# Batch 3's k turned by the transposing DMA in a kernel of sliding-window attention and a feed-forward layer

## The chip, the core and the metric

The kernel runs on one core of a Trainium2 chip. The core has a TensorE (PE in the profile; its weight loads are PEld), a VectorE (DVE), a ScalarE (ACT), a GpSimd (POOL) and a SyncE (SP), which here does nothing but issue DMAs. Each engine works off its own list of instructions in order; they meet through semaphores. SBUF is the on-chip memory, PSUM the banks that TensorE writes into. The metric is the device time of one execution in microseconds (us), as the median of several runs.

## What is computed

Eight batches, eight heads, 576 tokens, 64 values a head. Attention looks back over a window of 128 tokens with a linear bias that differs by head; its output, 4608 tokens of 512 values, is the x of a feed-forward layer.

```python
scores = scale * np.matmul(q, k.transpose(0, 1, 3, 2))
mask = (rel >= 0) & (rel < 128)                 # rel = row position - column position
scores = np.where(mask, scores + bias[None], -1000000000.0)
attn = softmax(scores)
x = np.matmul(attn, v)                          # then heads side by side: 4608 x 512
h = x @ w_in                                    # 512 x 2048
g = h * np.clip(h + 3.0, 0.0, 6.0) / 6.0
out = g @ w_out                                 # 2048 x 512, float32
```

Inputs and output are float32; matmuls take bfloat16.

## The kernel before

Attention goes in steps of two heads of one batch. A step has the number g: batch g // 4, pair g % 4, so g runs from 0 to 31. The feed-forward layer goes in nine tiles of 512 tokens. Its units are "ups" (`moe_up`: four matmuls over the four head pairs of x^T, then a Relu on ScalarE into `r6` and a multiplication on VectorE into `gbuf`) and "downs" (`moe_down`: four of the sixteen matmuls of a 128-token output block; after the fourth unit VectorE copies the block to `osb`, and SP writes it out). `fill(n)` places up to n of these units between the parts of an attention step. The order of every engine's instructions is written out by hand: the program stands in a manual schedule, and instructions run on each engine in the order in which the Python code issues them. An up whose tile needs a batch that is not yet finished is held back when the program is built (`done`), so which unit stands where is fixed too.

Scores need q and k with the head's values on the partitions: `qTb` and `kTb`, two buffers each, taken by turns by even and odd batches. x is needed the same way round: `xT`. There are two ways to turn something round:

- By TensorE: `double` transposes nine 128x128 blocks of a pair of head pairs (five, then four) from a cast copy `pr` into PSUM, and an engine copies the result into `qTb` or `kTb`.
- By the DMA: `xbar` (line 200) is one transposing DMA of 20 blocks from the cast copy `tbuf`; `back` (line 476) is one of five blocks from `avs`, the normalised output of a step, into `xT`. All of them are issued by SP, in line with the loads of q, k and v (line 112, five DMAs for a tensor of one batch) and the writes of the output (line 562).

From step 8 on, the loop in `segment` runs one iteration for each g. Iteration g issues scores of step g, with the masks and exponentials of g, the product of step g - 1 with v (`values`), the turning of g - 1's output (`back`), feed-forward units in between, and last `stage_next(g)`, which loads, casts and turns for the next batch. (Step 13's scores come at the end of iteration 12.) So q and k of batch 3 are got ready in iterations 8 to 11, those of batch 4 in 12 and 13.

Batch 3 is the odd one out. Its q is loaded in token order, cast by GpSimd into `tbuf` (iteration 9) and turned by one transposing DMA. Its k is loaded in runs of nine tokens (`load_double`), cast by GpSimd into two `pr` tiles in iterations 8 and 9 (`prepare_double`), and turned by TensorE in iterations 10 and 11: the dictionary `turn` in `segment` calls `double` twice in each, with a copy on ScalarE after each of the two parts. From batch 4 on, q and k are both cast into `tbuf`, q in the first iteration of the batch before and k in the second, and turned by one transposing DMA each; k's cast has to wait until q's turn has read `tbuf`.

SP's list around the change, from iteration 9 on, is: an output block; x^T of step 8; v of batch 3 (five loads); q of batch 3 turned; an output block; x^T of step 9; q of batch 4 (five loads); three output blocks; k of batch 4 (five loads); q of batch 4 turned; x^T of step 12; v of batch 4 (five loads); k of batch 4 turned; an output block; x^T of step 13; q of batch 5 (five loads); an output block; x^T of step 14; an output block; x^T of step 15; k of batch 5; and so on. (Steps 10 and 11 are turned back by TensorE.)

The tile 3 of the feed-forward layer is the first that needs batch 3. Its first up stands in iteration 17, after the scores of step 17, and reads x^T of steps 12 to 15.

Of the kernel before, what the change touches and what calls it, by code (L numbers as in the profile page):

```python
# [11 lines left out]
BF16 = mybir.dt.bfloat16  # L12
# [6 lines left out]
def kernel(  # L19
# [9 lines left out]
    nc = tc.nc  # L29
    B, H, S, D = q.shape  # L30
# [5 lines left out]
    NP = H // 2  # L36
    NQ = 5
# [3 lines left out]
    RP, RT = 64, 9  # L41
# [21 lines left out]
    bias_o = perm.tile([128, H], FP32)  # L63

    held = ctx.enter_context(tc.tile_pool(name="held", bufs=1))
    prs = ctx.enter_context(tc.tile_pool(name="prs", bufs=2))
    ppool = ctx.enter_context(tc.tile_pool(name="ppool", bufs=2))
    small = ctx.enter_context(tc.tile_pool(name="small", bufs=2))
    rpool = ctx.enter_context(tc.tile_pool(name="rpool", bufs=2))
# [4 lines left out]
    ps_o = ctx.enter_context(tc.tile_pool(name="ps_o", bufs=1, space=bass.MemoryType.PSUM))  # L74

    tbuf = held.tile([128, NP, NQ, 128], BF16, name="tbuf")
    ldbuf = [held.tile([128, NQ * H * D], FP32, name=f"ldbuf{i}") for i in range(4)]
    gbuf = [held.tile([128, n_ms, NT], BF16, name=f"gbuf{i}") for i in range(2)]
    vbuf = [held.tile([128, NQ, H, W], BF16, name=f"vbuf{i}") for i in range(2)]
    p4buf = [held.tile([128, 2, 128], BF16, name=f"p4buf{i}") for i in range(2)]  # L80
    qTb = [held.tile([128, NP, NQ, 128], BF16, name=f"qTb{i}") for i in range(2)]
    kTb = [held.tile([128, NP, NQ, 128], BF16, name=f"kTb{i}") for i in range(2)]
# [19 lines left out]
    def tokens(b, nm):  # L102
        if (b, nm) not in ld:
            i = 2 + b % 2 if b < 3 else (3, 1, 0, 2)[(3 * (b - 3) + "qkv".index(nm)) % 4]
            ld[b, nm] = ldbuf[i][:, 0:NQ * H * D].rearrange("p (j h d) -> p j h d", j=NQ, h=H)
        return ld[b, nm]

    def load_tokens(b, nm):
        t = tokens(b, nm)
        for j in range(NQ):  # L110
            n = min(128, S - j * 128)
            nc.sync.dma_start(out=t[:n, j, :, :],
                              in_=src_of[nm][b, :, ds(j * 128, n), :].rearrange("h p d -> p h d"))
# [66 lines left out]
    def cast_v(b, j, copy):  # L180
        n = min(128, S - j * 128)
        copy(out=vbuf[b % 2][:n, j, :, 0:D], in_=ld[b, "v"][:n, j, :, :])

    def cast_tokens(b, nm):
        s = ld[b, nm]
        if nm == "v":
            for lo in (0, 2):
                nc.gpsimd.tensor_copy(  # L188
                    out=vbuf[b % 2][:, lo:lo + 2, :, 0:D].rearrange("p j h d -> p (j h) d"),
                    in_=s[:, lo:lo + 2, :, :].rearrange("p j h d -> p (j h) d"))  # L190
            nc.gpsimd.tensor_copy(out=vbuf[b % 2][:LAST, 4, :, 0:D], in_=s[:LAST, 4, :, :])
            return
        for j in range(NQ):
            m = min(128, S - j * 128)
            nc.gpsimd.tensor_copy(out=tbuf[:m, :, j, :],  # L195
                                  in_=s[:m, j, :, :].rearrange("p (i e) d -> p i (e d)", e=2))

    def xbar(b, nm):
        dst = (qTb if nm == "q" else kTb)[b % 2]
        nc.sync.dma_start_transpose(out=dst.rearrange("p h j c -> p (h j) c"),  # L200
                                    in_=tbuf.rearrange("p h j c -> p (h j c)"))

    st = {}

    def prepare(g, copies):
        for nm, copy in zip("qk", copies):
            pr = prs.tile([128, RT * D], BF16, tag=f"pr{nm}", name="pr",
                          padded_shape=[128, 2 * RT * D])
            copy(out=pr, in_=runs[nm][:, g % NP, :])
            st[g, nm] = pr  # L210

    def transposes(g, copies):
        b, hp = divmod(g, NP)
        for nm, dst, copy in (("q", qTb[b % 2], copies[0]), ("k", kTb[b % 2], copies[1])):
            src = st.pop((g, nm))
            tp = ps_h.tile([128, RT, RP], BF16, tag="h", name="tp", padded_shape=[128, 16, 64])
            for t in range(RT):
# [3 lines left out]
            copy(out=dst[:, hp, :, :].rearrange("p j c -> p (j c)")[:, 0:S].rearrange(  # L221
                "p (a t) -> p a t", t=RT), in_=tp.rearrange("p t a -> p a t"))

    def prepare_double(b, dp, copies, nms="kq", early=None):
        for nm, copy in zip(nms, copies):
            pr = prs.tile([128, RT, 2 * D], BF16, tag=f"pr{nm}", name="pr2")
            for e in range(2):
                copy(out=pr[:, :, ts(e, D)],  # L228
                     in_=ldbuf["qk".index(nm)][:, ds((2 * dp + e) * RT * D, RT * D)].rearrange(
                         "p (t d) -> p t d", t=RT))  # L230
                if early and (nm, e) == (nms[0], 0):
                    early()
            st[b, dp, nm] = pr
# [3 lines left out]
    def double(b, dp, nm, part, tag, copy):  # L237
        src = st[b, dp, nm]
        t0, t1 = ((0, 5), (5, RT))[part]
        tp = BANKS[tag].tile([128, t1 - t0, 128], BF16, tag=tag, name="tp2",  # L240
                             padded_shape=[128, 8, 128])
        for t in range(t0, t1):
            nc.tensor.transpose(tp[:, t - t0, :], src[:, t, :], ident)  # L243
        dst = (qTb if nm == "q" else kTb)[b % 2][:, 2 * dp:2 * dp + 2, :, :]
        copy(out=dst.rearrange("p i j c -> p i (j c)")[:, :, 0:S].rearrange(  # L245
                 "p i (a t) -> p i a t", t=RT)[:, :, :, t0:t1],
             in_=tp.rearrange("p t (a i) -> p i a t", i=2))

    def wide_double(b, dp, nm, copy):
# [195 lines left out]
    def values(g, qts):  # L445
        av = ps_av.tile([128, 3, 2, W], FP32, tag="av", name="av", padded_shape=[128, 3, 2, 85])
        nq = len(qts)
        av_matmuls(g, qts, lambda qt, e: av[:, qt - qts[0], e, :])
        if qts[0] == 0:
            st[g, "avs"] = small.tile([128, NQ, 2, D], BF16, tag="avs", name="avs")  # L450
        rc = small.tile([128, 3, 2, 1], FP32, tag="rc", name="rc")
        nc.vector.reciprocal(rc[:, 0:nq, :, :], av[:, 0:nq, :, D:W])
        nc.vector.tensor_tensor(  # L453
            out=st[g, "avs"][:, qts[0]:qts[0] + nq, :, :], in0=av[:, 0:nq, :, 0:D],
            in1=rc[:, 0:nq, :, :].to_broadcast([128, nq, 2, D]), op=ALU.mult)
# [13 lines left out]
    def by_xbar(g):  # L469
        return g >= XB and g != XB + 2 and g != XB + 3  # L470
# [103 lines left out]
    def fill(n):  # L574
        for _ in range(n):
            if at[0] == len(units):
                return
            nt, fn, step = units[at[0]]
            if fn is moe_up and done[0] < NP * (min((nt * NT + NT - 1) // S, B - 1) + 1):
                return  # L580
            fn(nt if fn is moe_up else nt - 1, step)
            at[0] += 1

    V, P, A = nc.vector.tensor_copy, nc.gpsimd.tensor_copy, nc.scalar.copy

    LOADS = {9: "v3", 10: "q4", 12: "k4", 13: "v4", 14: "q5", 16: "k5", 17: "v5", 18: "q6",
             20: "k6", 21: "v6", 22: "q7", 24: "k7", 25: "v7"}

    VCAST = {15: 4, 19: 5, 23: 6, 27: 7}

    def stage_next(g):
        b, hp = divmod(g, NP)
        nb = b + 1
        if g == 2 * NP:
            cast_tokens(2, "v")
        for n in LOADS.get(g, "").split():
            load_tokens(int(n[1]), n[0])
        if nb == 3 and hp < 2:
            prepare_double(3, hp, (P,), "k")
        if nb == 3 and hp == 1:  # L600
            cast_tokens(3, "q")
            xbar(3, "q")
        elif nb < B and nb > 3 and hp < 2:
            cast_tokens(nb, "qk"[hp])
            xbar(nb, "qk"[hp])
        if VCAST.get(g):
            cast_tokens(VCAST[g], "v")

# [109 lines left out]
    def segment(lo, hi, fills):  # L718
        for g in range(lo, hi + 1):
            f = fills(g)  # L720
            if by_xbar(g - 2):
                done[0] = g - 1
            if lo < g < hi and g != 3 * NP + 1:
                scores(g)
            turn = {2 * NP: (2, 1, "k"), 2 * NP + 1: (2, 1, "q"),
                    2 * NP + 2: (3, 0, "k"), 2 * NP + 3: (3, 1, "k")}.get(g)
            if turn:
                double(*turn, 0, "av", A)
            fill(f[0])
            if turn:  # L730
                double(*turn, 1, *(("h", V) if turn[0] == 2 else ("av", A)))
            if g < hi:
                exp_diag(g, 0)
            fill(f[1])
            if g < hi:
                exp_diag(g, 1)
            if g == 3 * NP:
                cast_tokens(3, "v")
            if g > lo:
                values(g - 1, (0, 1, 2))  # L740
            fill(f[2])
            if g < hi:
                exp_off(g, 0)
            fill(f[3])
            if g < hi:
                exp_off(g, 1)
            if g > lo:
                values(g - 1, (3, 4))
            fill(f[4])
            if g > lo and by_xbar(g - 1):  # L750
                back(g - 1)
            fill(f[5])
            if g < hi:
                stage_next(g)
            fill(1)
            if g == 3 * NP:
                scores(g + 1)
            if g > lo and not by_xbar(g - 1):
                back(g - 1)
                done[0] = g  # L760
            fill(f[6] - 1)
# [51 lines left out]
```

## Time and profile before

| what | us |
|---|---|
| median of 3 runs | 321.99 |
| lowest and highest of them | 320.54, 322.87 |
| the profiled execution: time | 320.94 |
| the profiled execution: span of the instructions | 319.2 |
| PE busy | 310.1 |
| ACT busy | 195.7 |
| DVE busy | 173.1 |
| POOL busy | 141.2 |

The profiled execution took 1.7 us more than its span, which lies around the first and the last instruction, and 1.05 us less than the median of the runs. The profile counts a PE as busy while matmuls are in flight, so its share says that something was under way, not that the array worked at its peak. A line of the timeline gives the start and the length in us, the engine, the source line, the operation, the tile written and the tiles read, and how many instructions were merged. SP's lines are marked SPq: their length is the time for which SP was occupied with issuing the DMA, not the time until the data had landed, which another view gives ("DMA to landing", counted from the start of the issue).

### The profile page before, as it was taken

What the parts mean: (1) busy time and instruction counts of PE and PEld (TensorE: products, weight loads), DVE (VectorE), ACT (ScalarE), POOL (GpSimd) and SP (SyncE); (2) the same over time, 40 slices, a digit from 0 to 9 for tenths busy, and PEclk for the clock granted to TensorE, in tenths of its full rate; (3) what the DMA queues carried; (4) which work ended last, traced back from release to release, by engine and by line L of the source; (5) the groups of instructions that cost most, each with busy time, mean ns of one, the idle gap of its engine ahead of it and who ended that gap; (6) DMA issues with size and microseconds to landing.
All of it is one profiled execution on the core that took longest, in us unless ns stands there. A gap on an engine that the chain in (4) does not pass through costs nothing.

```text
span 319.2 us, 7124 instructions
## 1 busy us (share of the span) xinstructions
PE 310.1 (97%) x2775; PEld 164.9 (52%) x2775; DVE 173.1 (54%) x338; ACT 195.7 (61%) x334; POOL 141.2 (44%) x249
## 2 busy tenths in 40 slices
PE   7879999999999999999999999999999999999996
PEld 5565465455545454445677654444444444444443
DVE  6667675554355655655565556555656455455510
ACT  4748976877767776676676667666764344244401
POOL 8464493684496477266744673663331000000000
PEclk9999999999999999999999999999999999999999
DMA  7999999999999999998999999962212110000112
GB/s 281 199 323 225 256 260 195 249 231 194 215 252 157 239 208 211 205 222 194 207 205 211 209 190 196 225 93 68 38 39 88 53 36 33 33 33 35 66 56 75
DMA packets 131425, 51.90 MB, mean 163 GB/s; under 512 B 118976, under 2 KB 123328, under 8 KB 131392
## 3 DMA queue, kind: packets, MB, share of 16 engines
q1 hardware_dynamic: 126160, 45.36, 68.0%
q0 software_dynamic: 4224, 4.19, 8.2%
q10 hardware_dynamic: 1008, 1.90, 1.6%
q8 instruction: 21, 0.34, 0.5%
q14 instruction: 12, 0.10, 0.1%
HBM read 36.70 MB, written 9.44 MB: 145 GB/s over the span
## 4 chain that ended last, share of the span: by engine, by line
PE 86%; DMA 5%; ACT 4%; POOL 2%; DVE 2%; issue 1%; POOLq 0%
PE ops L552 38%; PE hps L502 36%; DMA w_in_sb<-in_moe_w_in_dram 3%; PE sce L365 3%; PE av L442 2%; PE av L434 2%; DMA ldbuf<-in_k_dram 2%; ACT r L521 2%; PE ops L533 1%; ACT kTb L245 1%; ACT gbuf L399 1%; PE tp L243 1%; DVE gbuf L522 0%; ACT gbuf L377 0%; PE tb L483 0%
## 5 line engine op out<-in xcount | busy, mean ns | idle before, releaser
L522 DVE SCALAR_TENSOR_TENSOR gbuf<-r,hps 128x512 bf16<-128x512 f32 x144 | 98.7, 688 | 101.0 <-ACT r L521 99.8
L521 ACT ACTIVATE r<-hps,bias 128x512 f32<-128x512 f32 x144 | 98.9, 689 | 86.8 <-PE hps L502 86.6
L502 PE MATMUL hps<-xT,w_in_sb 128*128 128x512 bf16 (+1 forms) x640 | 144.9, 358 | 0.6 <-ACT xT L489 0.3
L552 PE MATMUL ops<-w_out_sb,gbuf 128*128 128x512 bf16 x560 | 137.8, 379 | 0.0
L502 PEld LDWEIGHTS <-w_in_sb 128*128 128x128 bf16 x640 | 59.3, 98 | 55.0 <-issue 0.8
L552 PEld LDWEIGHTS <-gbuf 128*128 128x128 bf16 x560 | 51.9, 98 | 56.3
L415 POOL TENSOR_SCALAR_AFFINE_SELECT po<-po 128x512 bf16<-128x512 bf16 x48 | 30.3, 636 | 32.5 <-ACT po L413 32.4
L406 POOL TENSOR_SCALAR_AFFINE_SELECT pd<-pd 128x512 bf16<-128x512 bf16 x48 | 29.8, 634 | 33.5 <-ACT pd L389 33.5
L389 ACT ACTIVATE pd<-sce,bias_d 128x512 bf16<-128x512 f32 x48 | 31.7, 684 | 5.4 <-PE sce L373 2.7
L561 DVE COPY osb<-ops 128x512 f32<-128x512 f32 x33 | 22.7, 688 | 20.0 <-PE ops L552 17.5
L195 POOL CAST tbuf<-ldbuf 128x512 bf16<-128x512 f32 (+1 forms) x45 | 25.6, 614 | 16.8 <-issue 9.3
L413 ACT ACTIVATE po<-sce,bias_o 128x512 bf16<-128x512 f32 x48 | 33.0, 687 | 0.0
L453 DVE TENSOR_TENSOR avs<-av,rc 128x384 bf16<-128x384 f32 (+1 forms) x48 | 23.6, 491 | 1.6
L442 PEld LDWEIGHTS <-pd 128*128 128x128 bf16 x192 | 14.3, 97 | 8.3 <-issue 0.5
L434 PE MATMUL av<-vbuf,po 128*128 128x65 bf16 x192 | 18.0, 193 | 0.0
L442 PE MATMUL av<-vbuf,pd 128*128 128x65 bf16 x192 | 17.3, 193 | 0.3 <-ACT kTb L245 0.3
L434 PEld LDWEIGHTS <-po 128*128 128x128 bf16 x192 | 14.3, 98 | 2.9 <-DVE avs L453 0.5
L188 POOL CAST vbuf<-ldbuf 128x1024 bf16<-128x1024 f32 x14 | 14.2, 1043 | 3.5 <-DMA ldbuf<-in_v_dram 3.5
L418 ACT ACTIVATE p4buf<-sce,bias_d 128x64 bf16<-128x64 f32 x48 | 15.5, 323 | 0.0
L228 POOL CAST pr<-ldbuf 128x576 bf16<-128x576 f32 x20 | 12.9, 670 | 5.1 <-DMA ldbuf<-in_k_dram 3.1
L365 PE MATMUL sce<-qTb,kTb 64*64 64x192 bf16 (+1 forms) x368 | 11.9, 245 | 0.0
L365 PEld LDWEIGHTS <-kTb 64*64 64x64 bf16 x368 | 7.1, 106 | 8.6 <-issue 8.5
(104 smaller groups left out, 208.4 us busy)
## 6 DMA issues: line engine op xcount, KB each, us to landing
out_dram<-osb SPq DMA_DIRECT2D x33, 256.0 KB, 2.5
ldbuf<-in_v_dram SPq DMA_DIRECT2D x32, 256.0 KB, 5.2
ldbuf<-in_q_dram SPq DMA_DIRECT2D x20, 256.0 KB, 5.3
ldbuf<-in_k_dram SPq DMA_DIRECT2D x16, 256.0 KB, 4.4
ldbuf<-in_q_dram SPq DMA_DIRECT2D x12, 288.0 KB, 7.0
ldbuf<-in_k_dram SPq DMA_DIRECT2D x12, 288.0 KB, 6.3
w_in_sb<-in_moe_w_in_dram POOLq DMA_DIRECT2D x4, 512.0 KB, 9.2
w_out_sb<-in_moe_w_out_dram POOLq DMA_DIRECT2D x4, 512.0 KB, 10.3
```

Of the source, the lines that this page charges most:

```text
L195: nc.gpsimd.tensor_copy(out=tbuf[:m, :, j, :], in_=s[:m, j, :, :].rearrange("p (i e) d -> p i (e d)", e=2))
L365: nc.tensor.matmul(sce[e][lo:lo + 64, j, :, :].rearrange("p s c -> p (s c)")[:, ds(lo, n)], lhsT=kT[r, j, lo:lo + 64], rhs=qT[r, ds(128 * ...
L389: nc.scalar.activation(out=pd[:, e, :, :], in_=st["sce"][e][:, :, 0, :], func=ACT.Exp, bias=bias_d[:, h:h + 1], scale=scale)
L406: nc.gpsimd.affine_select(out=pd[:, e, :, :], in_=pd[:, e, :, :], pattern=[[0, 4], [1, 128]], channel_multiplier=-1, base=0, compare_op=AL ...
L413: nc.scalar.activation(out=po[:, e, :, :], in_=sc[:, :, 1, :], func=ACT.Exp, bias=bias_o[:, h:h + 1], scale=scale)
L415: nc.gpsimd.affine_select(out=po[:, e, :, :], in_=po[:, e, :, :], pattern=[[0, 4], [-1, 128]], channel_multiplier=1, base=-1, compare_op=A ...
L434: nc.tensor.matmul(out_av, lhsT=po[:, e, qt % 4 if full(g) else qt - 1, :], rhs=vb[:, qt - 1, h, :], start=True, stop=False)
L442: nc.tensor.matmul(out_av, lhsT=d, rhs=vb[:, qt, h, :], start=(qt == 0), stop=True)
L502: nc.tensor.matmul(hps[:, lo:hi], lhsT=w_in_sb[:, ks, ts(ms, 128)], rhs=xT[:, ks, ds(src, hi - lo)], start=(ks == 0), stop=(ks == n_ks - 1))
L521: nc.scalar.activation(out=r6, in_=hps, func=ACT.Relu, bias=bias3[:, 0:1], scale=1.0 / 6.0)
L522: nc.vector.scalar_tensor_tensor(out=gts[nt][:, ms, :], in0=r6, scalar=1.0, in1=hps, op0=ALU.min, op1=ALU.mult)
L552: nc.tensor.matmul(ops[nt, sub], lhsT=gts[nt][:, ms, ts(sub, 128)], rhs=w_out_sb[:, ms, :], start=(ms == 0), stop=(ms == n_ms - 1))
```

## The change

Four things change around batches 3 and later:

- k of batch 3 is no longer turned by TensorE. `turn_double` turns each of its two cast halves by a transposing DMA of nine blocks into a room of the same buffer, the first at the end of iteration 8 and the second at the end of iteration 10; `copy_double` puts the result in `kTb`, in one copy on ScalarE each, in iterations 11 and 13, before the off-diagonal exponentials.
- v of batch 3 is loaded in two parts, two loads before q's turn and three behind it.
- The `pr` tiles become one held buffer `prbuf` with four rooms. From batch 4 on, k is cast into the front of it (`tbuf2`) instead of `tbuf`, in the third iteration of the batch before, between the two diagonal exponentials (`turn_k`), instead of at the end of the second. Its unused corner is set to zero once.
- k of batch 4 is loaded in iteration 11 instead of 12.

SP's list becomes, from iteration 9 on: an output block; **k of batch 3, first half, turned**; x^T of step 8; v of batch 3 (two loads); q of batch 3 turned; v of batch 3 (three loads); an output block; x^T of step 9; q of batch 4 (five loads); **k of batch 3, second half, turned**; two output blocks; k of batch 4 (five loads); an output block; q of batch 4 turned; x^T of step 12; v of batch 4 (five loads); an output block; k of batch 4 turned; x^T of step 13; and from there as before, with k's turn behind the output block in each batch and not ahead of it. The order of the units on TensorE is the same as before without the 18 transposes; VectorE's list is unchanged.

```diff
+    prbuf = held.tile([128, 4, RT * 2 * D], BF16, name="prbuf")
+    tbuf2 = prbuf.rearrange("p n c -> p (n c)")[:, 0:NP * NQ * 128].rearrange(
+        "p (h j c) -> p h j c", h=NP, j=NQ)
...
+    def turned(b, nm):
+        return tbuf2 if b > 3 and nm == "k" else tbuf
...
-            nc.gpsimd.tensor_copy(out=tbuf[:m, :, j, :],
+            nc.gpsimd.tensor_copy(out=turned(b, nm)[:m, :, j, :],
...
+    def turn_double(b, dp, nm):
+        src = st.pop((b, dp, nm))
+        tp = st[b, dp, nm] = room_double(dp, "q")
+        nc.sync.dma_start_transpose(out=tp, in_=src.rearrange("p t c -> p (t c)"))
+
+    def copy_double(b, dp, nm, copy):
+        tp = st.pop((b, dp, nm))
+        dst = (qTb if nm == "q" else kTb)[b % 2][:, 2 * dp:2 * dp + 2, :, :]
+        copy(out=dst.rearrange("p i j c -> p i (j c)")[:, :, 0:S].rearrange(
+                 "p i (a t) -> p i a t", t=RT),
+             in_=tp.rearrange("p t (a i) -> p i a t", i=2))
...
-    LOADS = {9: "v3", 10: "q4", 12: "k4", 13: "v4", 14: "q5", 16: "k5", 17: "v5", 18: "q6",
+    LOADS = {10: "q4", 11: "k4", 13: "v4", 14: "q5", 16: "k5", 17: "v5", 18: "q6",
...
+    def turn_k(b):
+        if b == 4:
+            nc.gpsimd.memset(tbuf2[64:128, :, 4, :], 0.0)
+        cast_tokens(b, "k")
+        xbar(b, "k")
...
+        if nb == 3 and hp == 2:
+            turn_double(3, 1, "k")
         if nb == 3 and hp < 2:
             prepare_double(3, hp, (P,), "k")
+        if nb == 3 and hp == 0:
+            turn_double(3, 0, "k")
         if nb == 3 and hp == 1:
+            load_tokens(3, "v", range(0, 2))
             cast_tokens(3, "q")
             xbar(3, "q")
-        elif nb < B and nb > 3 and hp < 2:
-            cast_tokens(nb, "qk"[hp])
-            xbar(nb, "qk"[hp])
+            load_tokens(3, "v", range(2, NQ))
+        elif nb < B and nb > 3 and hp == 0:
+            cast_tokens(nb, "q")
+            xbar(nb, "q")
...
-            turn = {2 * NP: (2, 1, "k"), 2 * NP + 1: (2, 1, "q"),
-                    2 * NP + 2: (3, 0, "k"), 2 * NP + 3: (3, 1, "k")}.get(g)
+            turn = {2 * NP: (2, 1, "k"), 2 * NP + 1: (2, 1, "q")}.get(g)
...
+            if g % NP == 2 and 4 <= g // NP + 1 < B:
+                turn_k(g // NP + 1)
...
+            if g in (2 * NP + 3, 3 * NP + 1):
+                copy_double(3, g // NP - 2, "k", A)
```

More of the change, by code (lines that the diff above doesn't have):

```diff
@@ L65 @@
     held = ctx.enter_context(tc.tile_pool(name="held", bufs=1))
-    prs = ctx.enter_context(tc.tile_pool(name="prs", bufs=2))
     ppool = ctx.enter_context(tc.tile_pool(name="ppool", bufs=2))
@@ L106, in tokens, with load_tokens @@
         return ld[b, nm]
-    def load_tokens(b, nm):
+    def load_tokens(b, nm, blocks=range(NQ)):
         t = tokens(b, nm)
-        for j in range(NQ):
+        for j in blocks:
             n = min(128, S - j * 128)
@@ L200, in xbar @@
         nc.sync.dma_start_transpose(out=dst.rearrange("p h j c -> p (h j) c"),
-                                    in_=tbuf.rearrange("p h j c -> p (h j c)"))
+                                    in_=turned(b, nm).rearrange("p h j c -> p (h j c)"))
     st = {}
@@ L206, in prepare @@
         for nm, copy in zip("qk", copies):
-            pr = prs.tile([128, RT * D], BF16, tag=f"pr{nm}", name="pr",
-                          padded_shape=[128, 2 * RT * D])
+            pr = prbuf[:, 2 * "qk".index(nm) + g % 2, 0:RT * D]
             copy(out=pr, in_=runs[nm][:, g % NP, :])
@@ L222, in transposes, with room_double @@
                 "p (a t) -> p a t", t=RT), in_=tp.rearrange("p t a -> p a t"))
+    def room_double(dp, nm):
+        return prbuf[:, 2 * "qk".index(nm) + dp, :].rearrange("p (t c) -> p t c", t=RT)
     def prepare_double(b, dp, copies, nms="kq", early=None):
         for nm, copy in zip(nms, copies):
-            pr = prs.tile([128, RT, 2 * D], BF16, tag=f"pr{nm}", name="pr2")
+            pr = room_double(dp, nm)
             for e in range(2):
@@ L730, in segment @@
             if turn:
-                double(*turn, 1, *(("h", V) if turn[0] == 2 else ("av", A)))
+                double(*turn, 1, "h", V)
             if g < hi:
```

## Prediction

> **What bounds the kernel now.** I read the page's table of engines first, then the busy time by stretches.
>
> ```profile
> span 319.2 us, 7124 instructions
> PE 310.1 (97%) x2775; PEld 164.9 (52%) x2775; DVE 173.1 (54%) x338; ACT 195.7 (61%) x334; POOL 141.2 (44%) x249
> ```
> ```profile
> 92.00:124.00 32.00, 32.00 (x290) 16.02 (x289) 18.56 (x38) 22.61 (x42) 22.79 (x40) 1.00 1.12 205
> ```
>
> PE sets the end: 97% of the span, and all 32.00 of the 32 us after the stages that the change touches, at the full granted clock (1.00). No other engine is near. But in the same row the DMA share is 1.12, so the DMA engines are occupied without a pause too, at 205 GB/s. So the kernel stands on two legs: PE, and right beside it SP's list of DMAs. Next, SP's own timeline from iteration 9 (line 112 loads, 200 the turns of q and k, 476 x^T, 562 output).
>
> ```profile
> 68.39 0.56 SPq L562 DMA_DIRECT2D out_dram<-osb  x1
> 69.05 1.35 SPq L476 DMA_TRANSPOSE xT<-avs  x1
> 70.46 5.51 SPq L112 DMA_DIRECT2D ldbuf<-in_v_dram  x5
> 76.08 3.81 SPq L200 DMA_TRANSPOSE qTb<-tbuf  x1
> 80.40 0.38 SPq L562 DMA_DIRECT2D out_dram<-osb  x1
> 80.88 1.26 SPq L476 DMA_TRANSPOSE xT<-avs  x1
> 82.20 4.50 SPq L112 DMA_DIRECT2D ldbuf<-in_q_dram  x5
> 86.80 3.20 SPq L562 DMA_DIRECT2D out_dram<-osb  x3
> 90.06 4.50 SPq L112 DMA_DIRECT2D ldbuf<-in_k_dram  x5
> 94.77 3.85 SPq L200 DMA_TRANSPOSE qTb<-tbuf  x1
> ```
> ```profile
> 98.72 1.22 SPq L476 DMA_TRANSPOSE xT<-avs  x1
> 99.99 5.74 SPq L112 DMA_DIRECT2D ldbuf<-in_v_dram  x5
> 105.82 3.83 SPq L200 DMA_TRANSPOSE kTb<-tbuf  x1
> 109.75 0.53 SPq L562 DMA_DIRECT2D out_dram<-osb  x1
> 110.38 1.25 SPq L476 DMA_TRANSPOSE xT<-avs  x1
> ...
> 120.00 1.23 SPq L476 DMA_TRANSPOSE xT<-avs  x1
> ```
>
> Each row begins where the one before it ends, from 68 to 120 us: SP is backlogged. Only two holes show: 0.51 us ahead of 80.40 (76.08 + 3.81 = 79.89), and one inside the three output blocks at 86.80, which take 3.20 us where single ones follow each other at some 0.6 (109.75 to 110.38), so 3.20 - 1.8 = 1.4 us of waiting.
>
> **What TensorE gains.** The removed transposes are line 243 in PE's timeline of iteration 10; iteration 11 repeats them from 77.42.
>
> ```profile
> 69.28 0.45 PE L243 MATMUL tp<-ident,pr 128*128 128x128 bf16 x5
> 69.56 1.03 PE L502 MATMUL hps<-xT,w_in_sb 128*128 128x512 bf16 x4
> 70.58 0.38 PE L243 MATMUL tp<-ident,pr 128*128 128x128 bf16 x4
> 70.80 1.03 PE L552 MATMUL ops<-w_out_sb,gbuf 128*128 128x512 bf16 x4
> 71.99 0.22 PE L442 MATMUL av<-vbuf,pd 128*128 128x65 bf16 x2 [0.17 <-ACT kTb L245]
> ...
> 77.42 0.45 PE L243 MATMUL tp<-ident,pr 128*128 128x128 bf16 x5
> ...
> 80.14 0.22 PE L442 MATMUL av<-vbuf,pd 128*128 128x65 bf16 x2 [0.17 <-ACT kTb L245]
> ```
> ```profile
> 67.14 0.86 PE hps L502 x4
> ```
>
> The chain of waits gives 0.86 us for a group of four feed-forward matmuls. From 69.28 to 71.99 are 2.71 us, of which two such groups are 1.72: the turn costs 0.99 us, its transposes and the two waits on ScalarE's copy together. From 77.42 to 80.14 the same sum gives 2.72 - 1.72 = 1.00. Both go, and nothing replaces them on PE: **2.0 us** off PE's path, if nothing new holds it.
>
> **ScalarE, GpSimd, VectorE.** ScalarE loses four copies and gets two of 1152 columns. None of this kernel's ScalarE copies has that shape from SBUF; the nearest is the same copy out of PSUM:
>
> ```profile
> L257 ACT COPY kTb<-tp 128x1152 bf16<-128x1152 bf16 x1 | 1.1, 1112 | 0.0
> ```
>
> Taken at 1.1 us it costs nothing: ScalarE is busy 61% and iterations 10 and 11 lose more than they get; twice as much would still sit inside what was there. GpSimd's casts are the same instructions at another place, plus one small memset, on an engine busy 44%; k's cast no longer waits for q's turn to leave `tbuf`. I put both at zero; what they delay, the masks of one step, is wanted a step later.
>
> **What SP pays.** Two turns of nine blocks enter its list. Twenty blocks take 3.81 us of SP, five take 1.25 (rows at 76.08 and 110.38): a straight line gives 1.25 + 4 x (2.56 / 15) = 1.93 us for nine, 3.86 for both. Splitting v's loads and loading batch 4's k an iteration earlier reorder SP's list, with no more to issue; one output block, with its gap 0.63 us, now stands ahead of batch 4's k turn and not behind it. Who waits behind them? Everything SP issues, up to batch 4's k turn and to x^T of step 15. These have landed, counted from issue (first k's turn, then x^T):
>
> ```profile
> DMA to landing us min/median/max: 5.4/5.4/5.4
> ```
> ```profile
> DMA to landing us min/median/max: 3.1/3.1/3.1
> ```
>
> and this is when PE takes them up, in its timeline (scores of step 16, then the first up of tile 3):
>
> ```profile
> 112.50 0.52 PE L365 MATMUL sce<-qTb,kTb 64*64 64x192 bf16 x16
> ```
> ```profile
> 123.06 1.89 PE L502 MATMUL hps<-xT,w_in_sb 128*128 128x512 bf16 x8
> ```
>
> k lands at 105.82 + 5.4 = 111.2, so 1.3 us ahead of scores(16). x^T of step 15 lands at 123.1 and is first read by the fourth matmul of its group, at 123.06 + 3 x 0.86 / 4 = 123.7: 0.6 us of slack. Those are small cushions, and PE now wants both 2.0 us earlier.
>
> Let s be the delay of batch 4's k turn. Issued SP time adds 3.86 + 0.63 = 4.49. The two holes fill up, 0.51 + 1.4 = 1.9, leaving 2.6 as the upper end. Against it stands that SP's loads are slow because the DMA queue is full:
>
> ```profile
> L112 SPq DMA_DIRECT2D ldbuf<-in_q_dram x5: 568/938/1150, 82.2 to 85.6; - x5
> ```
>
> A load can be issued in 0.57 and takes 0.94 at the median. While SP issues a turn, the engines drain. A turn moves nine blocks of 32 KB, 295 KB, which at 205 GB/s is 1.44 us, so it leaves 0.5 us of room each, 1.0 in all; at the lower end its SP time is wholly paid back by loads that then go in at 0.57 (ten loads of q and k alone hold 10 x 0.37 = 3.7), and s falls to 2.6 - 3.7 = -1.1. I take **s = 1.6**, because the row of 205 GB/s is from this very stretch. On SP's time the Trainium skill speaks the other way: its page "DMA: Bandwidth & Descriptors", section "Issuing engines are not separate DMA queues", calls the time to initiate a DMA usually small relative to the DMA. By that rule s would be near its lower end and the 2.0 would be kept. The trace does not agree for the turns: 3.83 of 5.4 us are issue.
>
> **The sum.** k lands at 111.2 + 1.6 = 112.8. PE arrives at scores(16) at 112.5 - 2.0 = 110.5 and waits 2.3 us: more than it had gained, net 0.3 us late. x^T of step 15: the output block is again behind SP by then, so its delay is 1.6 - 0.6 = 1.0, against 0.6 of slack and PE 0.3 late: no more than 0.1 further. In general the change is s - 1.3, and never below -2.0. The profiled execution had 320.94 us (319.2 span and 1.7 around it), so it becomes 321.2; that execution lay 1.05 under the median of the runs, 321.99, and the time I give is for a median: **322.3 us**. What a measurement here tells from no change is about 1%, 3.2 us.
>
> **Rivals.**
> - *The gain stays (chance 0.27).* SP's new time is paid by loads that no longer stand before a full queue, s is between -1 and 0.7, and scores(16) waits at most 1.4: 2.0 to 0.6 faster, 320.0 to 321.4. For it: 0.94 against 0.57 in the row above, and the first turn stands where v's loads take 5.51 for five. Against it: the turn's own bytes go through the same engines, at a DMA share of 1.12. The rule just cited is this case.
> - *Turns cost more than their length (chance 0.20), slower.* A turn directly behind a turn is slow to land: x^T of step 12, issued at 98.72 straight behind q's turn, has this row,
>
> ```profile
> DMA to landing us min/median/max: 4.3/4.3/4.3
> ```
>
>  where step 15's took 3.1. The change makes such pairs: the first new turn and x^T of step 8, and from batch 4 on k's turn and x^T. With 1.2 us for each of two pairs ahead of PE's need, and no relief, s = 2.6 + 2.4 = 5.0: the sum 3.7 us slower, 325.7; with one pair, 2.5 slower, 324.5. It decides from s above 2.9. The Trainium skill points the same way in "VectorE: DVE Perf Modes", section "The three transpose paths": 390 ns for a 128x128 block on TensorE, 1309 ns on the DMA's crossbar. Its figure for 18 blocks would be an estimate of 24 us; the trace, 20 blocks landed in 5.4, does not agree with that size.
> - *ScalarE waits (chance 0.05).* ScalarE's timeline of iteration 13 has the two diagonal exponentials here:
>
> ```profile
> 93.12 1.26 ACT L389 ACTIVATE pd<-sce,bias_d 128x512 bf16<-128x512 f32 x2
> ```
>
>  The second turn is issued behind q4, at about 86.7 + 1.6, and lands within 5.4, by 93.7; the copy comes after these exponentials and one Relu, near 93 when PE is 2.0 earlier, with the Relus of the ups behind it. A wait of 1 to 2 us there would reach PE, but it takes from the same cushion that scores(16) eats: 322 to 324.
>
> **How the numbers follow.** The forecast, s from 0.7 to 2.9, has 0.48: 321.4 to 323.6. To hold 8 in 10 the range takes nearly all of the case with the gain kept and the lower half of the slower one: 320.0 to 324.4. Faster than 318.8 is beyond the 2.0 us that PE can gain, and left to scatter: 0.03. Slower than 325.2 is only the upper half of the second rival: 0.11. The rest, 0.86, is within 1%.
>
> **What would show it.** Line 243 loses 18 transposes and PE's gaps on line 245 in iterations 10 and 11 are gone. PE then waits on the DMA of `kTb` at scores(16), near 110.5 to 113. If that wait is missing and k's turn is issued before 106, the gain stayed. SP's new rows should be 1.9 us each; 3 us or more, or later x^T rows landing in over 4 us, speak for the second rival. An idle ScalarE ahead of the copy in iteration 13 speaks for the third. A wait of PE in iterations 12 to 15, on v or on q, would prove the place wrong.

## The result and the profile after

The changed kernel takes 324.75 us (median of 19 runs, 322.58 to 326.39), the kernel before 321.90 us (19 runs beside them): a ratio of 1.008, with a 95% interval of 1.0057 to 1.0103. It is slower by 0.8%, where 322.3 was forecast, and lies just above the range of 320.0 to 324.4. Ratios here and below leave out runs more than 1.5% above the fastest of their kernel, which are two of the twelve runs without the turns and no others. The profiled execution took 323.45 us, 2.51 more than the one before. First the head of its page.

```profile
span 321.7 us, 7041 instructions
PE 306.4 (95%) x2718; PEld 164.9 (51%) x2757; DVE 173.0 (54%) x338; ACT 197.1 (61%) x332; POOL 141.2 (44%) x250
```

PE is busy for 3.7 us less (310.1 before), and the span is 2.5 us longer. Not all of the 3.7 is work that went: the 18 transposes with their waits are 2.0, and the trace lacks some matmuls (2718 are recorded, beside 2757 weight loads). But PE now also waits. Where, its own timeline shows (start, length, engine, line, operation, tiles, count, and in brackets the idle time before and what ended it).

```profile
98.34 0.49 PE L384 MATMUL sce<-qTb,kTb 64*64 64x192 bf16 x15 [1.12 <-ACT p4buf L437]
...
114.34 0.52 PE L384 MATMUL sce<-qTb,kTb 64*64 64x192 bf16 x16 [1.62 <-DMA kTb<-prbuf]
...
126.43 1.24 PE L521 MATMUL hps<-xT,w_in_sb 128*128 128x512 bf16 x5 [0.71 <-DMA xT<-avs]
```

None of these three was there before: scores(14) waits for ScalarE, scores(16) for batch 4's k turn, the first up of tile 3 for x^T of step 15. A better measure than the bracket is the start of each step's scores in PE's timeline, counted from the start of scores(9). Up to there nothing is changed, and counting from there takes out that an execution starts half a microsecond earlier or later (61.12 before, 61.66 after).

| us from scores(9) to scores of step | 12 | 13 | 14 | 15 | 16 | 18 |
|---|---|---|---|---|---|---|
| before | 24.25 | 28.16 | 37.04 | 44.21 | 51.38 | 67.46 |
| after | 22.29 | 26.43 | 35.32 | 43.83 | 52.68 | 69.63 |
| difference | -1.96 | -1.73 | -1.72 | -0.38 | +1.30 | +2.17 |

Read the last row from left to right: 1.96 gained in iterations 10 and 11, 0.23 lost by step 13, 1.34 within iteration 14, 1.68 within iteration 15, 0.87 in iteration 17. From scores(18) on, the difference stays as it is.

Next SP's list, to be held against the two fences of it in the prediction.

```profile
69.69 2.26 SPq L259 DMA_TRANSPOSE prbuf<-prbuf  x1
72.04 1.22 SPq L495 DMA_TRANSPOSE xT<-avs  x1
73.31 1.21 SPq L114 DMA_DIRECT2D ldbuf<-in_v_dram  x2
74.62 4.67 SPq L205 DMA_TRANSPOSE qTb<-tbuf  x1
79.35 2.23 SPq L114 DMA_DIRECT2D ldbuf<-in_v_dram  x3
...
88.20 2.00 SPq L259 DMA_TRANSPOSE prbuf<-prbuf  x1
90.30 1.86 SPq L581 DMA_DIRECT2D out_dram<-osb  x2
92.22 4.92 SPq L114 DMA_DIRECT2D ldbuf<-in_k_dram  x5
97.23 0.66 SPq L581 DMA_DIRECT2D out_dram<-osb  x1
98.07 3.70 SPq L205 DMA_TRANSPOSE qTb<-tbuf  x1
...
103.15 5.18 SPq L114 DMA_DIRECT2D ldbuf<-in_v_dram  x5
108.43 0.57 SPq L581 DMA_DIRECT2D out_dram<-osb  x1
109.09 3.90 SPq L205 DMA_TRANSPOSE kTb<-prbuf  x1
...
123.08 1.23 SPq L495 DMA_TRANSPOSE xT<-avs  x1
```

From behind the output block ahead of x^T of step 8 to the issue of batch 4's k turn it is 109.09 - 69.69 = 39.40 us, and was 105.82 - 69.05 = 36.77 (the prediction's rows): 2.63 more. Of this the two turns with their gaps are 4.45 and the output block 0.66, together 5.1; the other items shrank by 2.5, most of all v's loads of batch 3 (1.21 + 2.23 in place of 5.51). The gap of 0.5 us ahead of the next output block is still there (79.35 + 2.23 = 81.58, and the block starts at 82.09). The k turn then lands in 5.2 us (5.4 before):

```profile
DMA to landing us min/median/max: 5.2/5.2/5.2
```

Last, ScalarE's timeline in iteration 13, with the second of the two new copies, and the two copies' durations (in ns: shortest, median, longest).

```profile
93.37 0.69 ACT L540 ACTIVATE r<-hps,bias 128x512 f32<-128x512 f32 x1 [0.19 <-PE hps L521]
93.95 2.18 ACT L264 COPY kTb<-prbuf 128x1152 bf16<-128x1152 bf16 x1
96.04 0.69 ACT L432 ACTIVATE po<-sce,bias_o 128x512 bf16<-128x512 f32 x1
...
97.96 0.33 ACT L437 ACTIVATE p4buf<-sce,bias_d 128x64 bf16<-128x64 f32 x1
```
```profile
L264 ACT COPY kTb<-prbuf x2: 2182/2196/2211, 80.4 to 94.0; 128x1152 bf16<-128x1152 bf16 x2
```

ScalarE does not wait for the turn: the copy begins right behind the Relu. But it takes 2.18 us, and `po` and `p4buf` of step 13 come only behind it. Scores(14) write the banks that these read; its second part, at 98.34, begins just after the `p4buf` of 97.96.

### The profile page after: what moved, and what is told of

Same layout as the page of the kernel before. It is cut to its first block, busy times and chain, and to the rows that moved or that the text cites. A ratio compares the mean times of both kernels' runs of the same rounds, so it can differ in the third digit from the quotient of the medians.

```text
span 321.7 us, 7041 instructions
## 1 busy us (share of the span) xinstructions
PE 306.4 (95%) x2718; PEld 164.9 (51%) x2757; DVE 173.0 (54%) x338; ACT 197.1 (61%) x332; POOL 141.2 (44%) x250
## 4 chain that ended last, share of the span: by engine, by line
PE 80%; DMA 10%; ACT 3%; issue 3%; POOL 2%; DVE 2%; SPq 0%; POOLq 0%; ACTq 0%
PE ops L571 34%; PE hps L521 33%; DMA w_out_sb<-in_moe_w_out_dram 5%; PE sce L384 3%; DMA ldbuf<-in_k_dram 2%; PE av L461 2%; DMA kTb<-prbuf 2%; PE av L453 2%; PE ops L552 1%; DMA xT<-avs 1%; PE w L155 1%; ACT r L540 1%; PE tp L224 1%; DVE gbuf L541 1%; POOL prbuf L235 1%
## 5 line engine op out<-in xcount | busy, mean ns | idle before, releaser
L521 PE MATMUL hps<-xT,w_in_sb 128*128 128x512 bf16 (+1 forms) x622 | 143.0, 357 | 2.6 <-DMA xT<-avs 0.7
L571 PE MATMUL ops<-w_out_sb,gbuf 128*128 128x512 bf16 x539 | 133.8, 379 | 2.7 <-issue 2.1
L235 POOL CAST prbuf<-ldbuf 128x576 bf16<-128x576 f32 x20 | 12.8, 668 | 6.5 <-DMA ldbuf<-in_k_dram 4.6
L200 POOL CAST tbuf<-ldbuf 128x512 bf16<-128x512 f32 (+1 forms) x25 | 14.2, 611 | 0.2 <-DMA ldbuf<-in_q_dram 0.2
```

Source lines behind the costliest of these rows:

```text
L521: nc.tensor.matmul(hps[:, lo:hi], lhsT=w_in_sb[:, ks, ts(ms, 128)], rhs=xT[:, ks, ds(src, hi - lo)], start=(ks == 0), stop=(ks == n_ks - 1))
L571: nc.tensor.matmul(ops[nt, sub], lhsT=gts[nt][:, ms, ts(sub, 128)], rhs=w_out_sb[:, ms, :], start=(ms == 0), stop=(ms == n_ms - 1))
```

## The experiments

The theory tested, S where an expectation uses a letter: TensorE's 2.0 us are real, and are spent where it waits for what the DMA list now brings later. Each expectation names the rivals that its run tells apart. All diffs are against the changed kernel; every run was timed with the kernel before beside it on the same chip.

**The turns taken out.** Neither turn nor copy is issued; batch 3 is left with an older k.

```diff
-        if nb == 3 and hp == 2:
-            turn_double(3, 1, "k")
...
-        if nb == 3 and hp == 0:
-            turn_double(3, 0, "k")
...
-            if g in (2 * NP + 3, 3 * NP + 1):
-                copy_double(3, g // NP - 2, "k", A)
```

> The changed kernel without the two new turns and the two ScalarE copies: batch 3 takes the k that batch 1 left in the buffer, so its k is neither turned by the DMA nor by TensorE. Theory S (SP's list with the two turns in it is late, and the copies hold ScalarE): both waits of PE in iterations 14 and 16 and the wait on x^T go, the gain of 2.0 us on PE is seen whole, about 320.0 where before has 322 (ratio 0.994). Rival R (the rest of the change costs: k's cast amid the masks, k's turn behind an output block): still 322 to 324, with a wait at scores(16).

Measured: 321.62 us, ratio 0.9983 (0.9956 to 1.0010). In its profiled execution, of 319.62 us, scores(18) come 65.91 after scores(9), 1.55 earlier than before, and one wait is left:

```profile
111.18 0.52 PE L384 MATMUL sce<-qTb,kTb 64*64 64x192 bf16 x16 [0.34 <-DMA kTb<-prbuf]
```

So even with nothing added to the list, a TensorE that is 2 us early runs into batch 4's k. The median lies 1.6 us over the 320.0 expected and shows no certain gain, and the 12 runs spread over 5 us (319.08 to 324.12); the section on the hardware comes back to that.

**TensorE's turns put back, without and with DMA work beside them.** In the first kernel the two halves of k go over TensorE as before, and the rest of the change stays. In the second the two DMA turns are issued as well, and nobody reads them. In the third, plain copies stand in their place, of eight blocks in pieces of 256 bytes.

```diff
-            turn = {2 * NP: (2, 1, "k"), 2 * NP + 1: (2, 1, "q")}.get(g)
+            turn = {2 * NP: (2, 1, "k"), 2 * NP + 1: (2, 1, "q"),
+                    2 * NP + 2: (3, 0, "k"), 2 * NP + 3: (3, 1, "k")}.get(g)
```
```diff
-        nc.sync.dma_start_transpose(out=tp, in_=src.rearrange("p t c -> p (t c)"))
+        nc.sync.dma_start(out=tp[:, 0:8, :], in_=src.rearrange("p t c -> p (t c)").rearrange(
+            "p (t c) -> p t c", t=8)[:, :, 0:128])
```

> As e1, with TensorE turning batch 3's k as before the change: the second buffer, the later cast of k, the parted loads of v and the earlier load of k remain. Theory S: within 0.6 us of before, 321.5 to 322.6, k of batch 4 landing no later than 112. Rival R: 323.5 or more, as the changed kernel.

> As e2, with the two DMA turns of nine blocks issued where the change has them, into a room that nobody reads; no copies on ScalarE. Theory S: PE waits at scores(16) on k of batch 4, which lands near 114, with no wait at scores(14); slower than e2 by 1 to 2.5 us, so 323 to 324.5. Rival A (the copies on ScalarE, 2.2 us each, are the whole cost): as e2, within 0.5.

> As e3, with a plain copy of eight of the nine blocks, in pieces of 256 bytes, in place of each DMA turn: nearly the same bytes and packets, without the turn's long issue. If SP's time of issue is what delays the list: as e2, within 0.5 us. If it is the DMA engines' work: as e3.

| TensorE turns k, and | median us | ratio (95%) | batch 4's k lands, us from scores(9) | scores(16), us from scores(9) |
|---|---|---|---|---|
| nothing beside | 321.85 | 1.0010 (0.9991 to 1.0028) | 51.2 | 51.34 |
| DMA turns unread | 323.99 | 1.0090 (1.0057 to 1.0123) | 53.0 | 53.01 |
| plain copies unread | 323.66 | 1.0058 (1.0027 to 1.0088) | 53.3 | 53.35 |

The rest of the change costs no time (1.0010), but only because TensorE is not early there: k lands 1.0 us later than in the kernel before (50.1), and 0.2 of its cushion is left. The two turns alone delay the k turn by 1.8 us more and cost 2.1. The third row says what in a turn costs this. (In its profiled execution the scores(9) themselves came 1.3 us late, behind a late load of w_out, so its last two columns count from a late start; its median does not depend on them.) First SP's timeline around the second turn, in the kernel with the turns unread, then around the second copy.

```profile
88.10 3.28 SPq L259 DMA_TRANSPOSE prbuf<-prbuf  x1
91.47 1.00 SPq L581 DMA_DIRECT2D out_dram<-osb  x2
...
98.20 3.70 SPq L205 DMA_TRANSPOSE qTb<-tbuf  x1
```
```profile
88.82 0.63 SPq L259 DMA_DIRECT2D prbuf<-prbuf  x1
89.55 2.92 SPq L582 DMA_DIRECT2D out_dram<-osb  x2
...
98.61 5.10 SPq L205 DMA_TRANSPOSE qTb<-tbuf  x1
```

The copy occupies SP for 0.63 us, the turn for 3.28, and yet the k turn lands as late: behind the copy the two output blocks take 2.92 for 1.00 and q's turn 5.10 for 3.7. The 2.65 us that SP saves it gives back. So a delay of this size comes without the long issue, from the work of the DMA engines. Their rate agrees: from 69 to 110 us they moved 211 GB/s in all three kernels, at a share of 1.16 to 1.18, so the added bytes took added time. Two turns are 0.59 MB, which at that rate is an estimate of 2.8 us. How much of a turn's own delay is its issue was not measured apart.

**The waits, one at a time.** Without batch 4's v (neither loaded nor cast), five loads fewer stand ahead of the k turn:

```diff
-            load_tokens(int(n[1]), n[0])
+            if n != "v4":
+                load_tokens(int(n[1]), n[0])
```

> The changed kernel without the five loads of batch 4's v and their cast: batch 4 takes the v of batch 2. Theory S (what counts is the work in line ahead of batch 4's k and of x^T): k of batch 4 lands some 5 us earlier, the waits of PE at scores(16) and at the first up of tile 3 go, the one at scores(14) stays; 321 or less, 1 to 2 under before. Rival C (the loss is the ScalarE copy, with the wait at scores(14)): still over 323.

Measured: 321.10 us, ratio 0.9984 (0.9967 to 1.0000). The waits at scores(16) and on x^T are gone, ScalarE's stays, and scores(18) come 67.29 after scores(9): 0.17 earlier than before. The gain in the median, 0.9 us, is just short of the 1 to 2 expected; the rival's 323 is ruled out.

```profile
98.17 0.49 PE L384 MATMUL sce<-qTb,kTb 64*64 64x192 bf16 x15 [1.12 <-ACT p4buf L437]
```

With the two copies on VectorE instead:

```diff
-                copy_double(3, g // NP - 2, "k", A)
+                copy_double(3, g // NP - 2, "k", V)
```

> The changed kernel with the two copies of batch 3's k on VectorE instead of ScalarE. Theory S: the wait at scores(14) goes, PE is 1.4 us earlier there and gives it all back at scores(16), where k of batch 4 lands as before; same time as the changed kernel, 324 to 325.5, and more runs with a reduced clock, the single wait being longer. Rival C: 1.4 us faster than the changed kernel, 323.4 or less.

Measured: 326.05 us, ratio 1.0118 (1.0094 to 1.0143), slower than the changed kernel and over the 324 to 325.5 expected. All four runs had a reduced clock, as the expectation had feared of some. Scores(14) and (15) come at 35.08 and 42.25, so the whole gain is there until iteration 15, and then one wait takes it all:

```profile
117.20 0.85 PE L384 MATMUL sce<-qTb,kTb 64*64 64x192 bf16 x16 [5.08 <-DMA kTb<-prbuf]
```

ScalarE's copy is a true delay, but in the changed kernel the later wait for k swallows it: taking it away gains nothing while k is late. Part of the 5.08 is that the list itself ran later in this execution, k's turn being issued at 110.71 and landing in 6.45; the change gives no reason for that, and it was not followed up.

With k of batch 4 and later cast at the end of the second iteration and turned ahead of v's loads:

```diff
+        if 4 <= nb < B and hp == 1:
+            turn_k(nb)
...
-            if g % NP == 2 and 4 <= g // NP + 1 < B:
-                turn_k(g // NP + 1)
```

> The changed kernel with batch 4's (and later) k cast at the end of the second iteration and turned ahead of v's loads, so some 5 us earlier in SP's list. Theory S: no wait at scores(16); what is late next is x^T of step 15, which stays where it was, so the wait at the first up of tile 3 grows to about 2.5: 323 to 324.5. Rival (k's turn is the only late thing): 321 or less.

Measured: 322.27 us, ratio 1.0011 (0.9993 to 1.0030), better than the 323 to 324.5 expected and short of the rival's 321. The wait at scores(16) is gone, and since the list behind it also moved up, x^T of step 15 holds PE for 0.62 us. ScalarE's wait is unchanged, and scores(18) come at 67.86, 0.40 later than before.

**SP relieved of output blocks, a miss.** The first eight output blocks were to be issued by ScalarE, to see what their SP time is worth.

```diff
-                nc.sync.dma_start(out=out[rows, :], in_=osb)
+                (nc.scalar if nt < 2 else nc.sync).dma_start(out=out[rows, :], in_=osb)
```

> The changed kernel with the eight output blocks of the first two tiles issued by ScalarE instead of SP: 0.6 us of SP's time each goes, the bytes stay. If the DMA engines' work is what the list waits for (as the plain copies suggested): k of batch 4 lands within 1 us of the changed kernel, 324 to 325.5. If SP's time of issue is: k lands 3 us earlier, 322 or less.

Measured: 328.62 us, ratio 1.0197 (1.0162 to 1.0231). It says nothing on SP, since ScalarE now stands in its own order waiting for the block that VectorE copies, and TensorE waits for ScalarE: scores(14) are 3.7 us later than before already.

**Orders meant to keep the gain.** K first and the copies on VectorE; then in addition two of the five loads of batch 5's q behind x^T of step 15; and, as a control, k first with TensorE's turns and no DMA turns.

```diff
+        if g == 16:
+            load_tokens(5, "q", range(3, NQ))
...
-            load_tokens(int(n[1]), n[0])
+            load_tokens(int(n[1]), n[0], range(3) if n == "q5" else range(NQ))
```

> The changed kernel with batch k turned ahead of v's loads (as in the earlier run where k came first) and with the two copies of the turned k on VectorE in place of ScalarE. Theory 'the gain of 2.0 us on TensorE is real and is spent in three waits': the waits at scores(14) and scores(16) are both absent, and only x^T of step 15 still holds TensorE, by 1.5 to 2.5 us now that TensorE comes there about 1.4 us earlier than in the run with k first, so that most of what is won there is lost again: 320.8 to 322.3. Rival 'the turns cost what they are worth through DMA contention everywhere, so no order of the list helps': 322.5 or more, with a new wait on a DMA before iteration 17.

> As the run with k first and the copies on VectorE, and batch 5's q has only three of its five blocks loaded ahead of x^T of step 15, the other two behind it. Theory 'three waits': x^T of step 15 is issued some 2.0 us earlier, the wait at the first up of tile 3 falls under 0.7 us, and 1.3 to 2.0 us of the gain are kept: 320.0 to 321.0, under the kernel before. Rival 'x^T is late for another reason (its own input, not the loads ahead of it)': the wait stays at 1.5 us or more, 321.5 to 322.5.

> Batch 3's k turned on TensorE as in the kernel before, with no DMA turns, and with k ahead of v's loads from batch 4 on. Tells apart what the order of the list gives by itself from what the turns give. Theory 'the order only serves a TensorE that comes early; in the kernel before it had slack there': 321.5 to 322.2, no change from before. Rival 'the order itself makes the kernel faster': 320.8 or less; then what the run with k first recovered is no measure of the turns.

| | median us | ratio (95%) | scores(16) | scores(18), us from scores(9) |
|---|---|---|---|---|
| k first, copies on VectorE | 322.47 | 1.0011 (0.9990 to 1.0032) | 49.43 | 68.28 |
| and q's loads parted | 321.91 | 0.9980 (0.9955 to 1.0004) | 49.42 | 67.38 |
| k first, TensorE's turns | 322.00 | 0.9983 (0.9962 to 1.0003) | 51.36 | 67.44 |

Both orders bring TensorE to scores(16) with the full 1.96 in hand, and both lose it in the two steps after, so both missed their range (320.8 to 322.3 and 320.0 to 321.0). The first one's rival had named a new wait on a DMA before iteration 17 as its sign, and there is one, in iteration 16; neither expectation had said which. The second one's timelines, of SP, VectorE and PE:

```profile
106.00 4.40 SPq L114 DMA_DIRECT2D ldbuf<-in_v_dram  x5
...
111.16 1.25 SPq L495 DMA_TRANSPOSE xT<-avs  x1
```
```profile
116.34 0.56 DVE L472 TENSOR_TENSOR avs<-av,rc 128x384 bf16<-128x384 f32 x1 [2.43 <-DMA xT<-avs]
```
```profile
116.96 0.20 PE L453 MATMUL av<-vbuf,po 128*128 128x65 bf16 x1 [1.70 <-DVE avs L472]
```

Now v's five loads, and no longer k's turn, stand just ahead of x^T of step 13, which lands 5.1 us after its issue, where it took 2.4 in the kernel before. That turn has not read `avs` when VectorE wants to overwrite it, VectorE keeps `av`, and TensorE waits 1.70 us for `av`. In each of the orders tried, the next thing in the list became the one that was late: x^T of step 15 with k first, x^T of step 13 with the copies on VectorE (and x^T of steps 14 and 15 too, where q's loads were not parted). The control shows that the order by itself is worth nothing that can be told from zero.

**Both legs relieved at once.** Batch 4's v left out and the copies on VectorE, the two edits above in one kernel.

> Batch 4's v is neither loaded nor cast (its values are left over from batch 2), so that five loads fewer stand ahead of batch 4's k turn, and the copies of the turned k are on VectorE. Theory 'TensorE's 2.0 us are real; the DMA list and ScalarE's copies take them back': none of the waits at scores(14), scores(16) and x^T of step 15 is left, from scores(9) to scores(18) it takes 65.3 to 65.7 us where the kernel before takes 67.46, and the time is 1.6 to 2.2 us under the kernel before, some 319.9 to 320.4. Rival 'what TensorE no longer does comes back in some other wait, whatever the list': 321 or more, as in the run with only v left out (321.1).

Measured: 319.61 us (319.45 to 320.48) against 322.23, ratio 0.9922 (0.9891 to 0.9952). Scores(18) come 65.51 after scores(9), and scores(16) find k there:

```profile
110.85 0.52 PE L384 MATMUL sce<-qTb,kTb 64*64 64x192 bf16 x16
```

That is 1.95 us of gain kept out of 1.96, and the median is even 2.6 lower, a little under the 319.9 to 320.4 expected. With five loads gone and ScalarE free, no other wait takes the place of the three. This kernel leaves work out, so it is no version to use; none of those that do all the work was surely faster than the kernel before.

## Why the prediction was wrong

- *TensorE's gain, 2.0 us*: right. 0.97 and 0.99 in iterations 10 and 11, and kept whole where the waits are removed.
- *SP's two turns, 1.93 us each*: nearly. 2.26 and 2.00, and each landed within 5.5 us.
- *s = 1.6, the delay of batch 4's k turn*: the term that failed first. Counted from scores(9), k landed at 50.1 us in the kernel before and at 52.6 in the changed one, so s was 2.5. Some 0.6 of the miss is the issued time (5.1 for 4.49, gaps and a slow first turn). The step behind the rest is "the two holes fill up": it took 1.9 us for them, and they gave 0.5. The first hole is still there, and the output blocks of the second take 0.5 less in all, not 1.4. That as much as 2.5 was paid back, near the 2.9 of the sum (1.9 and 1.0), is luck: batch 3's v loads alone gave 2.1, where the sum had 1.0 for all loads, and the other items about cancel. The holes were gaps in SP's list, not idle time of the DMA engines: in the kernel before, their busy share is 1.27 from 79.89 to 80.40 us and 1.26 from 86.8 to 90. Nor did they stand idle while SP issued the two new turns: their share was 1.13 from 69.7 to 71.9 us and 1.42 from 88.2 to 90.2. The run with plain copies shows that with less SP time the same delay remains. The Trainium skill's rule that issuing is the small part (the page "DMA: Bandwidth & Descriptors", section "Issuing engines are not separate DMA queues") agrees with that run, where 0.63 us of issue went with the whole delay. It did not lead to the kept gain that the first rival drew from it, because the DMA's own work was the cost.
- *The change is s - 1.3*: right as a rule. With 2.5 it gives 1.2, and scores(16) came 1.30 later.
- *x^T of step 15, "no more than 0.1 further"*: wrong by 0.8. The prediction let its delay fall to 1.0, because the output block is again behind SP by then, and put PE 0.3 late. It landed 62.0 us after scores(9) before and 64.7 after: 2.74 late. The output block's 0.6 did not come back, because the five loads of batch 5's q, between k's turn and this x^T, took 5.97 for 5.46. By the prediction's own slack of 0.6, with PE 1.30 late, 2.74 - 0.6 - 1.30 = 0.84; measured 0.87.
- *ScalarE's copies "cost nothing; twice as much would still sit inside"*: wrong in size, and hidden in effect. They took twice as much, and did not sit inside: 0.23 and 1.34 us of PE. The share of 61% was the wrong row to judge by; what counts is that `po` and `p4buf` stand behind the copy in the same iteration. The copy that gave the price of 1.1 has the same shape and the same order of reading and writing (line 257 before, line 264 in the changed kernel), but reads from PSUM:

```profile
L257 ACT COPY kTb<-tp x1: 1112/1112/1112, 25.2 to 25.2; 128x1152 bf16<-128x1152 bf16 x1
L257 ACT COPY qTb<-tp x1: 1122/1122/1122, 49.2 to 49.2; 128x1152 bf16<-128x1152 bf16 x1
```

 The prediction named that difference and put no time on it; from SBUF the copies took 2.18 and 2.21. In the changed kernel this loss shows in no total, because scores(16) wait for k anyway.
- *The rivals*: the gain did not stay. That turns cost more than their length gave a time near the measured one (324.5 with one pair), for another reason: the k turn landed in 5.2 us, not later than before, and x^T behind it was no slower (2.4 both times). Only x^T of step 8, behind the first new turn, landed slower, in 4.6 us for 3.5, and nothing waited for it. ScalarE waited for no turn, though by little: the second one landed at 93.7, and the copy began at 93.95.
- *The median*: 324.75 - 321.90 = 2.85, while the waits make 2.17. The rest no step of the prediction had; what may account for it stands under the hardware below.

## What to carry to other kernels

Here TensorE and SP's list ran side by side with a slack of 1.3 us between them, so work moved from TensorE to the list could gain no more than that slack, less the delay that it adds to the list. A prediction should price the later waits in the list (the x^T, the buffer that a turn frees) as carefully as the first. A gap in SP's list need not be idle time of the DMA engines: look at their share in that gap, and price a DMA beside a backlogged list by its bytes as well as by the time that its issue takes. Take the price of a copy from a row whose source lies in the same memory, not only from one of the same shape. To compare executions, count the starts of the repeating step from one that the change does not touch: the waits then read off as differences, free of the scatter at the start.

## What the runs showed of the hardware

- **A wait of 1.94 us was followed by half TensorE's clock.** The busy time by stretches of the run with plain copies, whose scores(16) waited 1.94 us (the columns after the busy times are granted clock, DMA share, GB/s):

```profile
114.00:116.00 2.00, 0.28 (x14) 0.28 (x18) 0.69 (x1) 0.51 (x1) 2.00 (x4) 1.00 0.99 224
116.00:120.00 4.00, 3.84 (x34) 1.89 (x28) 0.00 (x0) 1.26 (x2) 1.22 (x3) 0.58 0.95 194
120.00:124.00 4.00, 4.00 (x26) 1.91 (x25) 2.63 (x5) 2.78 (x7) 1.22 (x2) 0.99 1.00 208
```

 From 116.65 the clock was 0.5 for 3.41 us, and from scores(16) to scores(17) took 9.70 us where the kernel before takes 8.04: 1.7 us more for a wait that was already over. The run with the copies on VectorE had a dip of the same length, which began 0.4 us before its wait of 5.08 us was over, and the run with output blocks on ScalarE had one behind two waits of 1.65 and 0.54 us with 0.24 us of work between them. No dip followed 1.58, 1.62 and 1.70 us. The Trainium skill ("TensorE: Matmul & The Clock Gate", Part 1) ties the half rate to an idle window of about 3.4 us on a free-running count. The length of the dips agrees with that, but an idle time of 1.94 us sufficed here.
- **Such dips may account for the rest of the median.** One lowers the mean clock of a run by 0.5 x 3.41 / 322 = 0.005. Of the changed kernel's 19 runs, 9 have a mean clock of 0.995, with 325.2 us on average; the other ten have 1.0 and 324.0, which is 2.1 over the kernel before, as the waits say. The two groups overlap, though: three of the ten took 325.5 to 326.4 at the full clock. The kernel without the turns has a low clock in 5 of 12 runs, with 323.1 us on average against 320.7 for the others, which is why its median hides the gain. Of the 85 runs of the kernel before beside the experiments, 2 are under 0.997. That the dip of each of these runs stands behind a wait is not shown: there is one profile of each kernel, and the one without the turns, at the full clock, shows no wait from scores(9) on that is longer than 0.34 us.
- **The same copy took ScalarE 2.2 us from SBUF and 1.1 from PSUM**, with the same shape and order of elements. VectorE took 1.55 to 1.92 from SBUF, and 1.35 from PSUM:

```profile
L264 DVE COPY kTb<-prbuf x2: 1548/1735/1922, 82.2 to 95.4; 128x1152 bf16<-128x1152 bf16 x2
L257 DVE COPY qTb<-tp x2: 1351/1355/1359, 23.8 to 32.2; 128x1152 bf16<-128x1152 bf16 x2
```

 Not every read from SBUF is that slow: a cast of 576 columns in a row, from SBUF (line 209 of the kernel before), took ScalarE 0.67 us. The copy reads every 128th element; that this stride is what costs was not tested, nor was the work that ran beside it at the time.
- **A turn of nine blocks costs the list no more than a plain copy** of eight blocks in pieces of 256 bytes (medians of 323.99 and 323.66 us; k landed at 53.0 and 53.3).
